# A transformer block on one core: the last shifted reading of a shared key tile, added in int32 pieces on GpSimd

## The chip, the core and the metric

The kernel runs on one core of a Trainium2 chip. The metric is the device time of one execution in microseconds. The engines are TensorE (PE in the profile; PEld is its weight load), VectorE (DVE), ScalarE (ACT), GpSimd (POOL) and SyncE (SP, which here only issues DMAs). "Lnnn" is a line of the kernel before.

## What is computed

The input is x, 2048 rows of 512 bfloat16 numbers, and a conditioning vector c. Two stages follow one another:

```python
mod = (_silu(c) @ w_mod)            # six vectors: sa, ca, ga, sb, cb, gb
h = _layernorm(x) * (1 + ca) + sa
x = x + ga * _A_ref(h, A_wqkv, A_wo)     # 32 heads of 16, softmax(q k^T / 4) v, then wo
h = _layernorm(x) * (1 + cb) + sb
x = x + gb * _B_ref(h, B_w1, B_b1, B_w2, B_b2)   # gelu(h w1 + b1) w2 + b2, F = 1376
```

Nearly all elementwise work is the softmax's exponential: 32 heads x 2048 queries x 2048 keys.

## The kernel before

**Units, tiles, runs.** Queries are cut into four blocks of 512, keys into 16 tiles of 128. A unit is one score product, 128 keys by 512 queries of one head (`qk`, L822). Four heads that lie in four row groups of TensorE go together: four units are a key tile of a run, and a run (32 of them) is four heads against all 16 key tiles of one query block. In the last query block a run takes eight heads and half of the queries, in pieces of 256 columns. The value products of a run (`pv_op`, L960) add into one PSUM bank `od`; when all are in, `normalise` copies it out (L985), sends the sums of the weights through DRAM to turn them round and invert them, and multiplies on GpSimd (L1012).

**Two ways to the exponential.** ScalarE takes units in turns of three and two (`qk_a`): the scores go to the PSUM tiles `st`, and one activation (L871) writes bfloat16 weights `pt`. Each tile then costs one value product. VectorE takes whole tiles, four of the 16 in each run (`DKS`; one in run 0), in another way (`qk_d`, `shifts`). Four passes (L912), one for each unit, read the scores from PSUM (`ax`), add a constant and write int16 numbers `ph`, whose bits read as bfloat16 are a rough exponential. Four shifts (L927) over all four units, 2048 columns, each add an integer step `PH_SH[j]` in SBUF and write `sh`: five readings in all, and a value product for each, with values scaled by `PH_W[j]` (`VX`), averages the error out. A tile that VectorE has not begun when ScalarE has done its own 12 goes to ScalarE (`next_tile`).

**The order.** Nothing runs in the order of the source. While the kernel is built, a planner (`Plan`, `Op`) keeps for each engine a list of operations with assumed times, latencies and priorities, and always emits the one that can start first; among those close together the lowest priority value goes (`dyn`), with a small scatter from `SEEDS`. That order is fixed in each engine's queue. `ahead` lets nothing on TensorE come in the way of the next scores for ScalarE. `heat` puts zero matmuls into gaps where less than `HEAT` us of products stand in the last 3.4 us. An operation marked `port` (shifts, some VectorE work in SBUF, GpSimd's work) is planned to start only when the other of VectorE and GpSimd is not in such an operation.

**GpSimd beside VectorE.** `beside` (L1043) makes the multiplications of L1012 and L1035 (weights scaled by a gate) run on GpSimd; it has them work in halves of 256 columns, which the planner admits only while VectorE is in an operation that is not marked `port`; `after_dve` makes it wait for the VectorE instruction before the latest one in the queue, so that it starts when the latest starts.

**Tail blocks.** After the last run of a query block `block_tail` does the output projection (L1117), the residual (L1166), the second layer norm, W1 (L1183) with its evictions on VectorE (L1193), one gelu over the block (L1202) and W2 (L1123). For the last block it takes only two row tiles of four, and the first 8 of 11 columns of W1 that way; the other three wait until all units are done and go through ScalarE's gelu out of PSUM (L1189). `last_half` does the other two row tiles when all runs are over: it loads x again (L491), transposes `od` on VectorE to find the divisors (L1249 to L1256), finishes the projection (L1263), and goes through the residual (L1267), statistics, W1 (L1295), gelu (L1298), W2 and the last addition (L1310), one row tile after the other.

Of the kernel before, what the change touches and what calls it, by code (L numbers as in the profile page):

```python
# [12 lines left out]
ALU = mybir.AluOpType  # L13
# [40 lines left out]
PEL = 0.24  # L54
OVER = 0.0
DVE_PE = 0.0
DL = 0.14
DPL = 0.08
AL = 0.17
FILL = 1.6  # L60
SPREAD = 0.15
SEEDS = (571, 338, 517, 702, 966, 607, 659, 937, 623, 185, 209, 513, 12, 512, 674, 785, 660, 579, 642, 245, 112, 195, 497, 319, 388, 80, 556, 716, 338, 990, 290, 195)
HEAT = 1.3
# [10 lines left out]
class Op:  # L74
    count = 0

    def __init__(self, eng, fn, us, deps=(), lat=0.14, prio=5.0, mode=None, kind="", acq=None,
                 rel=(), gate=None, port=False):
        self.port = port
        self.eng, self.fn, self.us, self.lat, self.prio = eng, fn, us, lat, prio  # L80
        self.mode, self.kind, self.acq, self.rel, self.gate = mode, kind, acq, rel, gate
        self.end = None
        self.ready = 0.0
        self.tile = None
        self.slot = None
        self.kb, self.due, self.extra = 0, 1e9, False
        self.uses = 0
        self.rows, self.cont, self.run = None, False, None
# [12 lines left out]
        for owner in rel:  # L101
            owner.uses += 1


class Plan:
# [56 lines left out]
    def ahead(self, can):  # L162
# [4 lines left out]
        limit = max(q[0][0], self.need() - q[0][1].us - PEL - 0.02) + OVER  # L167
# [90 lines left out]
def kernel(  # L258
# [34 lines left out]
    MM = 512 / 2400.0  # L293
# [55 lines left out]
    def dyn(plan, o):  # L349
        if o.eng == "DVE" and o.run is not None and (  # L350
                o.run < a_run[0] or o.run == a_run[0] and not own[o.run]):
            return 0.05
        if o.eng != "PE":
            return o.prio
# [14 lines left out]
        if o.kind == "last":  # L369
            return o.prio + 0.1 * same  # L370
        if o.due <= prog():
# [52 lines left out]
    warm = const.tile([P, P], BF16, name="warm")  # L424
    o_warm = op("POOL", lambda o: nc.gpsimd.memset(warm, 0.0), 0.2, prio=-1.0)
# [209 lines left out]
    def layer_norm(src, deps, mod, mod_dep, hold_z, alloc_h, engines, ps_res, kind, prio,  # L635
# [39 lines left out]
        else:  # L675
            for j in range(NC):
                def tr(o, j=j):
                    o.ps = o.tile.bitcast(BF16)[:, 0:nt * P]
                    for t in range(nt):
                        nc.tensor.transpose(out=o.ps[:, t * P:(t + 1) * P],  # L680
                                            in_=z.tile[:, t, j * P:(j + 1) * P], identity=ident)
                one = op("PE", tr, nt * 0.0705, za, lat=PEL, mode=("full", 0), kind=kind,
                         acq=r_ax, rel=(z,))
                trs.append(one)
                e = engines[j]
                done.append(op(e, lambda o, j=j, one=one, e=e: modulate(
                    e, h.tile[:, j, 0:nt * P], one.ps, mod, j), 0.13 + nt * 0.1, (one, mod_dep, h), prio=0.1,
                    rel=(one,)))
# [144 lines left out]
    def qk_a():  # L833
# [30 lines left out]
        o = op("PE", go, MM, deps, lat=PEL, mode=("qk",) + tuple(u[2] for u in got), kind="qkA", acq=r_st[n],  # L864
# [19 lines left out]
    def qk_d():  # L884
# [29 lines left out]
        d_e.append(op("DVE", ex, 0.61, (o,), lat=DL, prio=0.5, rel=(o,)))  # L914
# [7 lines left out]
    def shifts(r, kt, first, es):  # L922
# [3 lines left out]
        for j in range(1, NPH):  # L926
# [4 lines left out]
            pv_op(r, kt, j, (sh,), parts(sh), (sh,))  # L931

# [50 lines left out]
    def normalise(r):  # L983
# [20 lines left out]
        def d5(o):  # L1004
# [8 lines left out]
            out=OT.tile[:, c], in0=OD.tile[:, c], in1=o5.tile[:, c], op=ALU.mult), (OT,), (OD, o5))  # L1013
# [29 lines left out]
    def beside(fn, deps, rel=(), prio=0.5):  # L1043

        return [op("POOL", lambda o, c=c: after_dve(fn(slice(c * HB, (c + 1) * HB))), POOL_US, deps, lat=0.1,
# [107 lines left out]
    def block_tail(b, nt=TPB):  # L1153
# [19 lines left out]
        if part:  # L1173
            g.uses += 1
            o_late["part"] = g
            one = ones(g, (g,))
        ev = []
        over = op("NIL", None, 0.0, (), lat=0.0, prio=0.0, gate=finished) if part else None
        if part:
            open_banks()  # L1180
        for f in range(NF):
            direct = part and f >= PSUM_F
            mm = chain([(lambda ps, f=f, j=j: nc.tensor.matmul(  # L1183
                out=ps[:, 0:N], lhsT=W1[:, j, f * P:(f + 1) * P], rhs=h.tile[:, j, 0:N],
                start=(j == 0), stop=(j == NC - 1)), nt * MM / NC) for j in range(NC)],
                hd + [o_late["w1"], g, over if direct else None], kind,
                r_t if direct else r_ax, (h,))
            if direct:
                ev.append(op("ACT", lambda o, f=f, mm=mm: nc.scalar.activation(  # L1189
                    out=g.tile[0:rows(f), f, 0:N], in_=mm.tile[0:rows(f), 0:N], func=ACT.Gelu_apprx_tanh,  # L1190
                    bias=b1c[0:rows(f), f:f + 1], scale=1.0), 0.36, (mm,), lat=0.15, prio=0.4, rel=(mm,)))
                continue
            ev.append(op("DVE", lambda o, f=f, mm=mm: nc.vector.tensor_scalar(  # L1193
                out=g.tile[:, f, 0:N], in0=mm.tile[:, 0:N], scalar1=b1c[:, f:f + 1], scalar2=None,
                op0=ALU.add), 0.13 + nt * 0.134, (mm, o_late["b1"]), prio=0.3 if part else 0.1, rel=(mm,)))
# [13 lines left out]
        for t in range(nt):  # L1209
# [7 lines left out]
            dma(lambda o, t=t, a=a: nc.sync.dma_start(  # L1217
                out=out[0][b * QB + t * P:b * QB + (t + 1) * P, :], in_=a.tile), (a,), kb=128,
                rel=(a,))
        due(1e9)  # L1220


    def last_half():
        r, b = NR - 1, LAST
        full = ("full", 0)
        xr = load_x(b)
# [3 lines left out]
        x2 = xr  # L1230
        ln, z, h = take(r_ln, (x2,)), take(r_z, (x2,)), take(r_blk, (x2,))
        g = o_late["part"]
        od, OD, OT = o_od[r], take(r_OD), take(r_OT)
# [6 lines left out]
        s = None  # L1240
        for n, t in enumerate(tiles):
            den = work.tile([P, 8], FP32, name=f"den{t}")

# [3 lines left out]
            def turned(n):  # L1247
                return OD.tile[:, n * HB:(n + 1) * HB].rearrange("p (a q) -> p a q", a=2)
            sh = op("DVE", lambda o, t=t, half=half: nc.vector.transpose(out=turned(0), in_=half(od.tile)), 0.35,  # L1249
                    (o_last[r], OD, s), prio=0.06 + n)  # L1250
            rc = op("DVE", lambda o, den=den: nc.vector.reciprocal(
                out=den, in_=OD.tile[:, 16:HB:32]), 0.12, (sh,), prio=0.05 + n)
            bk = op("DVE", lambda o, den=den: nc.vector.transpose(
                out=turned(1).rearrange("p a q -> p (a q)"),
                in_=den.unsqueeze(2).to_broadcast([P, 8, 32])), 0.35, (rc,), prio=0.045 + n)
            ml = [op("DVE", lambda o, t=t, half=half: nc.vector.tensor_tensor(  # L1256
                out=half(OT.tile), in0=half(od.tile), in1=turned(1), op=ALU.mult),
                0.36, (bk, OT), prio=0.04 + n)]

            def wo2(o, t=t):  # L1260
                for p in range(2):
# [3 lines left out]
            w = op("PE", wo2, 2 * MM,  # L1265
                   ml + [early[t]], lat=PEL, mode=full, kind="last", prio=0.2)
            a = op("DVE", lambda o, t=t: nc.vector.tensor_tensor(  # L1267
                out=x2.tile[:, t, :], in0=acc[t].tile, in1=xr.tile[:, t, :], op=ALU.add), 0.62,
                (w, x2, xr), prio=0.024 + n / 50, rel=(acc[t],))
            s = op("DVE", lambda o, t=t: stats(ln, t, x2.tile[:, t, :]), 0.83, (a, ln), prio=0.022 + n / 50)  # L1270
            rs = op("POOL", lambda o, t=t: rstd(ln, t, t + 1), 0.9, (s,), prio=0.0)
            za = op("DVE", lambda o, t=t: apply(ln, z, t, x2.tile[:, t, :]), 0.33, (rs, z),
# [4 lines left out]
            for e in ("DVE", "ACT"):  # L1277
# [8 lines left out]
                for n, j in enumerate(js):  # L1286
                    hd.append(op(e, lambda o, n=n, j=j, e=e, at=at, tro=tro: modulate(
                        e, h.tile[:, j, at], tro.ps[:, n * P:(n + 1) * P], modB, j), 0.25, (tro, h),
                        prio=0.02, rel=(tro,)))
            gs = slice(HB + (t - 2) * P, HB + (t - 1) * P)  # L1290
            gd = []
            for f in range(NF):
                def w1(o, f=f, at=at):
# [3 lines left out]
                mm = op("PE", w1, 4 * 0.071, hd, lat=PEL, mode=full, kind="last", acq=r_t, prio=0.3)  # L1297
                gd.append(op("ACT", lambda o, f=f, mm=mm, gs=gs: nc.scalar.activation(  # L1298
                    out=g.tile[0:rows(f), f, gs], in_=mm.tile[0:rows(f), 0:P], func=ACT.Gelu_apprx_tanh,
                    bias=b1c[0:rows(f), f:f + 1], scale=1.0), 0.25, (mm,), prio=0.3, rel=(mm,)))  # L1300
            first = prev = None
            for f in range(NF):
                def w2(o, f=f, gs=gs):
                    w2_mm((first_of[id(o)] or o).tile, g.tile, gs.start, f, f + 1)
                o = op("PE", w2, MM, (gd[f], prev), lat=PEL if f == NF - 1 else 0.0, mode=full,
                       kind="last", acq=r_t if f == 0 else None, prio=0.4)
# [6 lines left out]
            dma(lambda o, t=t, a=a: nc.sync.dma_start(  # L1313
                out=out[0][b * QB + t * P:b * QB + (t + 1) * P, :], in_=a.tile), (a,), kb=128,
                rel=(a,))
# [137 lines left out]
```

## Time and profile before

| what | value |
|---|---|
| runs | 788.27 us median of 3 (787.38 to 789.58) |
| profiled execution, first to last instruction | 785.5 us |
| TensorE busy | 731.1 us (93%), 8209 matmuls |
| VectorE busy | 737.5 us (94%), 1285 instructions |
| ScalarE busy | 756.9 us (96%), 683 instructions |
| GpSimd busy | 125.0 us (16%), 279 instructions |
| share of the chain that ended last | ScalarE 42%, TensorE 29%, VectorE 14%, issue 12%, DMA 2% |
| end of the last exponential | 760.99 us |
| zero matmuls, L447, L431 | 11.2 us (116), 9.5 us (25) |

The profiled execution has no other time on record than its span; the median of the runs lies 2.8 us above it. In the page, a row such as `DVE 6779...` cuts the span into 40 slices of 19.6 us and gives the busy share of each in tenths. A group row has the line, the engine, what is written from what, the shapes, the count, the busy time and the mean length of one instruction, then the idle time in front of them and what ended it. A matmul's length includes its way through the array, and neighbours overlap; VectorE's and ScalarE's records overlap their neighbours too (a pass lasts 680 ns and the next one starts 600 ns after it).

### The profile page before, as it was taken

What the parts mean: (1) busy time and instruction counts of PE and PEld (TensorE: products, weight loads), DVE (VectorE), ACT (ScalarE), POOL (GpSimd) and SP (SyncE); (2) the same over time, 40 slices, a digit from 0 to 9 for tenths busy, and PEclk for the clock granted to TensorE, in tenths of its full rate; (3) what the DMA queues carried; (4) which work ended last, traced back from release to release, by engine and by line L of the source; (5) the groups of instructions that cost most, each with busy time, mean ns of one, the idle gap of its engine ahead of it and who ended that gap; (6) DMA issues with size and microseconds to landing.
All of it is one profiled execution on the core that took longest, in us unless ns stands there. A gap on an engine that the chain in (4) does not pass through costs nothing.

```text
span 785.5 us, 20448 instructions
## 1 busy us (share of the span) xinstructions
PE 731.1 (93%) x8209; PEld 272.8 (35%) x8286; DVE 737.5 (94%) x1285; ACT 756.9 (96%) x683; POOL 125.0 (16%) x279
## 2 busy tenths in 40 slices
PE   8899999999999898999998999999999999999897
PEld 3423333233333222223232233322234343344454
DVE  6779998999999999999999999999899999999974
ACT  4899999999999999999999999999999999999993
POOL 7420224121134300200002000001000100100100
PEclk9999999999999999999999999999999999999999
DMA  7042001001020010001000010001010000101010
GB/s 215 30 138 89 18 23 46 23 16 26 6 71 22 25 42 23 19 22 29 22 23 18 30 34 22 11 16 33 23 57 20 22 20 19 43 18 31 18 44 29
DMA packets 39073, 28.22 MB, mean 36 GB/s; under 512 B 17957, under 2 KB 34374, under 8 KB 38978
## 3 DMA queue, kind: packets, MB, share of 16 engines
q1 hardware_dynamic: 38970, 26.91, 12.0%
q8 instruction: 65, 1.06, 0.6%
q14 instruction: 30, 0.25, 0.1%
q10 hardware_dynamic: 8, 0.00, 0.0%
HBM read 21.30 MB, written 2.61 MB: 30 GB/s over the span
## 4 chain that ended last, share of the span: by engine, by line
ACT 42%; PE 29%; DVE 14%; issue 12%; DMA 2%; SPq 0%; POOL 0%; POOLq 0%; DVEq 0%; ACTq 0%
ACT pt L871 40%; PE od L960 9%; PE st L822 8%; DVE sh L927 6%; DVE ph L912 5%; PE ax L1123 2%; PE ax L822 2%; PE ax L1183 2%; ACT g L1202 1%; PE ax L701 1%; PE ax L431 1%; PE ax L740 1%; DVE ln_s L607 1%; DVE OD L985 1%; PE t L1123 1%
## 5 line engine op out<-in xcount | busy, mean ns | idle before, releaser
L871 ACT ACTIVATE pt<-st 128x1536 bf16<-128x1536 f32 x629 | 715.1, 1308 | 3.9 <-PE ax L822 1.7
L912 DVE TENSOR_SCALAR ph<-ax 128x512 int16<-128x512 f32 x476 | 311.1, 680 | 11.2 <-PE ax L822 9.7
L927 DVE TENSOR_SCALAR sh<-ph 128x2048 int16<-128x2048 int16 x476 | 310.8, 692 | 2.6 <-PE od L960 2.3
L822 PE MATMUL st<-qm,kT 32*128 32x512 bf16 x1572 | 246.8, 384 | 23.9 <-ACT pt L871 18.7
L822 PE MATMUL ax<-qm,kT 32*128 32x512 bf16 x476 | 167.0, 380 | 7.6 <-DVE ph L912 5.6
L960 PE MATMUL od<-sh,VX 128*32 128x512 bf16 (+1 forms) x2400 | 167.5, 340 | 5.4 <-DVE sh L927 4.6
L822 PEld LDWEIGHTS <-kT 32*128 32x128 bf16 x2048 | 81.1, 91 | 239.4 <-issue 230.6
L960 PE MATMUL od<-pt,VEB 128*32 128x512 bf16 (+1 forms) x1960 | 145.3, 342 | 0.3 <-ACT pt L871 0.3
L960 PEld LDWEIGHTS <-VX 128*32 128x32 bf16 x2400 | 60.5, 95 | 86.2 <-issue 75.3
L960 PEld LDWEIGHTS <-VEB 128*32 128x32 bf16 x2560 | 62.5, 96 | 75.6 <-issue 63.8
L1012 POOL TENSOR_TENSOR OT<-OD,RB 128x256 bf16<-128x256 f32 x38 | 27.2, 727 | 316.3 <-DVE sh L927 200.4
L960 PE MATMUL od<-ph,VEB 128*32 128x512 bf16 (+1 forms) x600 | 47.5, 340 | 1.7 <-DVE OD L985 1.4
L1012 POOL TENSOR_TENSOR OS<-OD,RB 128x256 bf16<-128x256 f32 x24 | 17.2, 727 | 156.7 <-DVE sh L927 111.0
L1183 PE MATMUL ax<-blk,W 128*128 128x512 bf16 (+1 forms) x145 | 39.8, 359 | 1.8 <-issue 0.6
L756 POOL TENSOR_SCALAR VX<-VEB 128x128 bf16<-128x128 bf16 x64 | 23.1, 360 | 80.7 <-DVE VEB L633 76.9
L701 PE MATMUL ax<-blk,w 128*128 128x512 bf16 x95 | 31.8, 382 | 3.7 <-DVE blk L626 0.9
L1123 PE MATMUL ax<-w,g 128*128 128x512 bf16 x100 | 29.2, 382 | 1.0 <-DVE ph L912 0.2
L1193 DVE TENSOR_SCALAR g<-ax,b1c 128x512 bf16<-128x512 f32 (+1 forms) x41 | 28.2, 692 | 1.1 <-PE ax L1183 0.7
L607 DVE BATCH_NORM_STATS2 ln_s<-xb 128x6 f32<-128x512 bf16 x32 | 21.6, 675 | 1.2 <-DMA xb<-in_A_x_dram 1.1
L1123 PEld LDWEIGHTS <-g 128*128 128x128 bf16 x176 | 14.0, 97 | 23.2 <-issue 12.7
L985 DVE COPY OD<-od 128x512 f32<-128x512 f32 x31 | 21.1, 681 | 0.7 <-issue 0.5
L1183 PEld LDWEIGHTS <-W 128*128 128x128 bf16 x176 | 14.0, 97 | 20.6 <-issue 14.9
(110 smaller groups left out, 367.5 us busy)
## 6 DMA issues: line engine op xcount, KB each, us to landing
RB<-rn SPq DMA_DIRECT2D x124, 64.0 KB
xb<-in_A_x_dram SPq DMA_DIRECT2D x8, 512.0 KB
out_dram<-o SPq DMA_DIRECT2D x16, 128.0 KB
qm<-qs SPq DMA_DIRECT2D x120, 16.0 KB
W<-in_B_w_dram SPq DMA_DIRECT2D x1, 1376.0 KB
w<-in_A_wqkv_dram SPq DMA_DIRECT2D x3, 384.0 KB
blk<-in_w_mod_dram SPq DMA_DIRECT2D x2, 512.0 KB
xb<-in_w_mod_dram SPq DMA_DIRECT2D x2, 512.0 KB
```

What stands on the lines that cost most here:

```text
L607: nc.vector.bn_stats(out=st6, in_=src)
L701: return chain([(lambda ps, j=j: nc.tensor.matmul(out=ps[:, 0:QB], lhsT=w.tile[:, j, cc * P:(cc + 1) * P], rhs=o_h[b].tile[:, j, :], start ...
L822: nc.tensor.matmul(out=o.tile[:, k * QB:(k + 1) * QB], lhsT=kT[cc][kb][rows, ko * P:(ko + 1) * P], rhs=qm.tile[rows, par, :] if hb is None ...
L871: nc.scalar.activation(out=e.tile[:, 0:len(got) * QB], in_=o.tile[:, 0:len(got) * QB], func=ACT.Exp, scale=ESC)
L912: nc.vector.tensor_scalar(out=ph.tile[:, o.row * QB:(o.row + 1) * QB], in0=o.tile, scalar1=PH_B, scalar2=0.0, op0=ALU.add, op1=ALU.max)
L927: sh = op("DVE", lambda o, j=j: nc.vector.tensor_scalar(out=o.tile, in0=first.tile, scalar1=PH_SH[j], scalar2=None, op0=ALU.add), 0.6, es, ...
L960: nc.tensor.matmul(out=o_od[r].tile[32 * i:32 * i + 32, n * HB:n * HB + w], lhsT=v_tile(kt, ph)[:, c0:c0 + 32], rhs=got[i][:, at:at + w], ...
L985: OD = op("DVE", lambda o: nc.vector.tensor_copy(out=o.tile, in_=od.tile), 0.6, (last,), prio=0.0, acq=r_OD, rel=(od,))
L1012: two = beside(lambda c: nc.gpsimd.tensor_tensor(out=OT.tile[:, c], in0=OD.tile[:, c], in1=o5.tile[:, c], op=ALU.mult), (OT,), (OD, o5))
L1123: nc.tensor.matmul(out=ps, lhsT=g[:, f, col:col + P], rhs=rhs, start=(f == 0), stop=(f == NF - 1))
L1183: mm = chain([(lambda ps, f=f, j=j: nc.tensor.matmul(out=ps[:, 0:N], lhsT=W1[:, j, f * P:(f + 1) * P], rhs=h.tile[:, j, 0:N], start=(j == ...
L1193: ev.append(op("DVE", lambda o, f=f, mm=mm: nc.vector.tensor_scalar(out=g.tile[:, f, 0:N], in0=mm.tile[:, 0:N], scalar1=b1c[:, f:f + 1], s ...
```

## The change

One of the four shifts of a VectorE tile, the last (`j = 4`), is no longer one VectorE instruction. `shared_reading` cuts it into four pieces of 512 int16 columns. GpSimd may add a piece as 256 int32 numbers, with the step in both halves of each (`PH_SH[-1] * 65537`); the planner admits a piece where `fits` finds a place beside VectorE's passes over PSUM. What GpSimd has not taken when VectorE comes to it, one VectorE instruction does (`rest`), late if a `ph` buffer is free and early if none is. TensorE's picks get a second filter, `fed`, which keeps other products from delaying VectorE's next scores.

Other parts go with it. The planner's assumed times of the exponentials now count to the end of the chain (`A_US`, `AL`, `PEA`), `HEAT` goes from 1.3 to 1.5, and the seeds are others. In tail blocks several transposes or W1 columns share a PSUM bank (only where fewer than 512 columns are used, for W1), and in the last block all 11 columns of W1 are done by VectorE's way before the runs end. `last_half` keeps the x tile that `block_tail` loaded, each of its two row tiles has an `OD` tile of its own, and the multiplication of the last run but one is not tied to a VectorE instruction.

```diff
+PEA = 0.38
 OVER = 0.0
+FEED = 0.2
...
-AL = 0.17
+AL = 0.055
...
-HEAT = 1.3
+HEAT = 1.5
...
-            can = self.ahead(can)
+            can = self.fed(self.ahead(can))
...
+    def fed(self, can):
+
+        q = [(s, o) for s, o in can if o.kind == "qkD"]
+        if not q:
+            return can
+        dry = self.free["DVE"] + sum(o.us for o in self.lists["DVE"])
+        limit = max(q[0][0], dry - q[0][1].us - PEL - DL) + FEED
+        return [(s, o) for s, o in can if o.kind in ("qkA", "qkD") or
+                s + o.us + (0.107 if o.mode[0] != "qk" else 0.0) <= limit]
...
+    def fits(self, us):
+
+        at, end, port = self.dve
+        t = max(at, self.now, self.free["POOL"])
+        if port and t < end:
+            return False
+        nxt = self.pick("DVE")
+        if nxt is None or nxt[0] - t >= us:
+            return True
+        if t >= end or nxt[0] > end + 0.15:
+            return not nxt[1].port and nxt[0] + nxt[1].us - t >= us
+        return end - t >= us or not nxt[1].port and nxt[0] + nxt[1].us - t >= us
...
-    A_US = {1: 0.49, 2: 0.92, 3: 1.345}
+    A_US = {1: 0.49, 2: 0.9165, 3: 1.3435}
+    PIECE = 0.74
+    REST = (4.0, 1.0)
+    PIECE_FIT = 0.6
...
-    PSUM_F = 8
+    PSUM_F = 11
...
+        if o.rest:
+            return REST[min(r_ph.free) > plan.now]
...
+    pair_sh = const.tile([P, 1], I32, name="pair_sh")
+    o_pair = op("POOL", lambda o: nc.gpsimd.memset(pair_sh, PH_SH[-1] * 65537), 0.1, prio=0.2)
...
-        for j in range(1, NPH):
+        shared_reading(r, kt, first, es)
+        for j in range(1, NPH - 1):
...
+    def shared_reading(r, kt, first, es):
+
+        sh = op("NIL", None, 0.0, es, lat=0.0, prio=0.0, acq=r_sh)
+        todo = [0, 1, 2, 3]
...
+        def add_pairs():
+            at = slice(todo[0] * QB, (todo[0] + 1) * QB)
+            del todo[:1]
+            return nc.gpsimd.tensor_tensor(out=sh.tile[:, at].bitcast(I32), in0=first.tile[:, at].bitcast(I32),
+                                           in1=pair_sh[:, 0:1].to_broadcast([P, HB]), op=ALU.add)
...
+        def part(o):
+            after_dve(add_pairs())
...
+        def rest(o):
+            o.us = (0.067, 0.2, 0.335, 0.47, 0.6)[len(todo)]
+            o.waiters.append(done)
+            add(len(todo))
+            drop()
...
+        mine = [op("POOL", part, PIECE, (sh, o_pair), lat=0.12, prio=0.8, kind="beside", port=True,
+               gate=lambda: plan.fits(PIECE_FIT)) for _ in range(4)]
+        q = op("DVE", rest, 0.6, (sh,), lat=DL, prio=2.0, port=True)
...
-            out=OT.tile[:, c], in0=OD.tile[:, c], in1=o5.tile[:, c], op=ALU.mult), (OT,), (OD, o5))
+            out=OT.tile[:, c], in0=OD.tile[:, c], in1=o5.tile[:, c], op=ALU.mult), (OT,), (OD, o5), free=r == NR - 2)
...
-        for f in range(NF):
-            direct = part and f >= PSUM_F
...
+        for f0 in range(0, NF, QB // N):
+            fs = range(f0, min(NF, f0 + QB // N))
...
-        xr = load_x(b)
+        x2 = held["x"]
...
-        s = None
         for n, t in enumerate(tiles):
             den = work.tile([P, 8], FP32, name=f"den{t}")
+            OD = take(r_OD)
```

More of the change, by code (lines that the diff above doesn't have):

```diff
@@ L87, in __init__ @@
         self.uses = 0
-        self.rows, self.cont, self.run = None, False, None
+        self.rows, self.cont, self.run, self.rest = None, False, None, False
         self.waiters = []
@@ L370, in dyn @@
             return o.prio + 0.1 * same
+        if o.cont:
+            return 0.9 + same
         if o.due <= prog():
@@ L1041, in w2_scaled, with beside @@
                       gb_bc, (W2[0], W2[1], o_late["small"], o_late["gb"]))
-    def beside(fn, deps, rel=(), prio=0.5):
+    def beside(fn, deps, rel=(), prio=0.5, free=False):
+        if free:
+            return [op("POOL", lambda o, c=c: fn(slice(c * HB, (c + 1) * HB)), POOL_US, deps, lat=0.1, prio=0.1,
+                       rel=rel, port=True) for c in range(2)]
         return [op("POOL", lambda o, c=c: after_dve(fn(slice(c * HB, (c + 1) * HB))), POOL_US, deps, lat=0.1,
@@ L1312, in last_half @@
                 acq=r_o, rel=(first,))
-            dma(lambda o, t=t, a=a: nc.sync.dma_start(
-                out=out[0][b * QB + t * P:b * QB + (t + 1) * P, :], in_=a.tile), (a,), kb=128,
-                rel=(a,))
+            store(b, t, a)
     first_of = {}
```

134 lines of the change are left out of this document (77 added, 57 removed).

## Prediction

> **What bounds the kernel now.** I read the page first: busy shares, the row of slices, the costliest groups.
>
> ```profile
> PE   8899999999999898999998999999999999999897
> DVE  6779998999999999999999999999899999999974
> ACT  4899999999999999999999999999999999999993
> L871 ACT ACTIVATE pt<-st 128x1536 bf16<-128x1536 f32 x629 | 715.1, 1308 | 3.9 <-PE ax L822 1.7
> L912 DVE TENSOR_SCALAR ph<-ax 128x512 int16<-128x512 f32 x476 | 311.1, 680 | 11.2 <-PE ax L822 9.7
> L927 DVE TENSOR_SCALAR sh<-ph 128x2048 int16<-128x2048 int16 x476 | 310.8, 692 | 2.6 <-PE od L960 2.3
> L822 PE MATMUL st<-qm,kT 32*128 32x512 bf16 x1572 | 246.8, 384 | 23.9 <-ACT pt L871 18.7
> ```
>
> ScalarE (ACT) is full from the second slice to the last but one, and its exponentials wait 3.9 us in all: **the exponentials on ScalarE set the end**, behind a head and a tail. VectorE (DVE) is just as full, and the two share one stock of work: 2048 units of 512 columns, four to a key tile. ScalarE does 1572 (715.1 us, 0.455 us each, 1.82 us a tile), VectorE 476, that is 119 tiles, each with four passes over PSUM (L912) and four shifts (L927): 621.9 / 119 = 5.23 us. Only 4 tiles of a run (one in the first run) may go to VectorE, 31 x 4 + 1 = 125. Six went back to ScalarE because VectorE was late; counting the loads of the scaled values between the ends of runs, they lie scattered, one run at a time. So a faster VectorE is worth **at most 6 x 1.82 = 10.9 us**, however much it is relieved.
>
> Then the timeline, where GpSimd (POOL) already multiplies 256 columns beside a pass:
>
> ```profile
> 155.07 0.68 DVE L912 TENSOR_SCALAR ph<-ax 128x512 int16<-128x512 f32 x1
> 155.24 0.73 POOL L1012 TENSOR_TENSOR OT<-OD,RB 128x256 bf16<-128x256 f32 x1 [16.53 <-DVE sh L927]
> 155.68 0.84 DVE L927 TENSOR_SCALAR sh<-ph 128x2048 int16<-128x2048 int16 x1
> 156.44 0.68 DVE L912 TENSOR_SCALAR ph<-ax 128x512 int16<-128x512 f32 x1
> ```
>
> The pass is untouched (0.68 us beside POOL as elsewhere); the shift behind it takes 0.84 us instead of 0.68, because POOL's 0.73 us reach over the pass's end. That is the price to watch.
>
> Last, the chain of waits behind the last exponential (it ends at 760.99 us):
>
> ```profile
> 758.76 1.43 POOL OT L1012 x2
> ...
> 762.67 3.80 DMA xb<-in_A_x_dram
> ...
> 766.59 0.70 DVE xb L1267
> ...
> 771.72 0.70 DVE xb L1267
> ...
> 776.09 2.63 PE t L1295 x44
> 778.73 0.05 issue
> 778.78 3.20 PE t L1123 x14
> ```
>
> Here 24.5 us lie outside ScalarE's bound: the multiply comes late, the x load is queued behind its DMAs on SP's queue, and the first addition (766.59) waits for the load.
>
> **The change, part by part.** Everything is set against the span of 785.5 us; the median of the runs, 788.27, lies 2.8 above it, and I add 2.8 at the end.
>
> *The fifth reading.* Per tile it removes one shift, 0.60 us of VectorE by the starts of neighbouring instructions, and puts up to four pieces of 256 int32 columns on POOL and one instruction for what is left on VectorE. No row shows an int32 add. The nearest are L1012 (727 ns, two float32 inputs) and L1035 (671 to 736 ns, bf16), both 256 columns with two inputs; I take 727, with bounds of 671 and, for the doubled output bytes, 1454. POOL is busy 125 us of 785.5, and 476 pieces would add 346: there is room. What costs is VectorE's wait. Of the 476 passes, 181 are followed at once by a shift and 198 by another pass; a piece in front of a second pass is free, one in front of a shift costs 0.16 to 0.21 us (837 and 893 ns against 680). Over what POOL does beside passes today (62 + 34 instructions at L1012 and L1035), 55 shifts average 112 ns longer: 6.2 us, 64 ns a piece. No row shows a quarter shift either: between 0.15 us (a quarter of 0.60) and 0.32 (the pitch of L618, 512 columns in SBUF); I take 0.20. If three pieces of four find a place, a tile saves 600 - 200 - 3 x 64 = 208 ns; bounds: 600 (all four, free) and 600 - 320 - 3 x 155 = -185. Over 119 tiles: **24.8 us of VectorE, from 71 down to -22**. I choose the middle because pieces want four passes a tile and find about five, 96 of all passes being taken by the older multiplies.
>
> *What that buys.* Below, three more evictions cost VectorE 1.4 us. (24.8 - 1.4) / 5.2 = 4.5 of the six tiles come back: **4.5 x 1.82 = 8.2 us** off ScalarE; bounds 10.9 gained and 22 / 5.2 x 1.82 = 7.7 lost. TensorE (PE) pays four more value products per tile, 4 x 0.39 us: 7 us inside its 54 us of idle time.
>
> *The wait that is added.* TensorE's value product of the fifth reading now waits for POOL or for the rest. Behind it on TensorE stand the next score products, and ScalarE waits for those. Today such waits on shifts come to 4.6 us in 17 cases (0.27 each) and ScalarE's exponentials lose 3.2 us to TensorE. 119 times 0.27 would be 32 us of TensorE; ScalarE has two score tiles in hand (0.92 and 1.34 us of work), which cover 0.27. I take nothing, with a bound of another 3.2 us. The pending reading also holds one of four buffers for shifts; VectorE waits 2.3 us for those today, and passes stand in.
>
> *More zero matmuls, new latencies.* The granted clock is 1.00 in every window from 60 us on, so nothing is to be won there; between 40 and 60 us it is 0.91, but ScalarE is busy 19.75 of the 20. Zero products at L447 and L431 take 20.7 us; half as many again stays inside TensorE's idle time. Nothing, with a bound of 1 us either way for a score product that stands behind one. The constant's memset on POOL costs 0.25 us by L553's rows, in the head; I take nothing. The latencies and seeds only reorder, and ScalarE's 3.9 us of waiting bound a gain.
>
> *The tail.* Three of eleven W1 products (12 matmuls, 1.48 us at 761.38) move ahead of the last exponential: TensorE has cover there, VectorE pays 3 x 0.478 = 1.4 us. The second x load goes, and the multiply of the last run but one no longer waits for a place. The first addition can then stand behind its product (OT's multiply, L1256, ends at 763.16, two products take 0.6), about 764.0 instead of 766.59; the second half's transposes no longer wait for the first's statistics, so its addition can come 3 us earlier too. What is late next is TensorE: from 761.38 to 781.98 it is idle only some 1.8 us. Without the 1.48 us it can end at most 1.48 + 1.8 = 3.3 us earlier. I take **2.0 us**, between nothing and 3.3, since the first W2 products still wait for the gelu.
>
> Sum: 785.5 - 8.2 - 2.0 = 775.3 us; with 2.8, **778.1**.
>
> **Rivals.**
> - *VectorE ceases to matter.* If pieces sit mostly in rows of passes, all six tiles return: 785.5 - 10.9 - 2.5 + 2.8 = 774.9. For it: 198 passes followed by a pass already, more of them with a quarter fewer shifts. Against: evictions of the tail blocks fall into bursts in which six late tiles arose.
> - *The relief doesn't arrive.* Pieces end late, the rest runs on VectorE, and only the tail is left: 785.5 - 2.0 + 2.8 = 786.3. For it: VectorE has hardly any idle time in which to be early, and a run's tiles can't be begun much ahead. Against: a saved 0.6 us needs no gap.
> - *Slower: the port.* If pieces fall in front of shifts, each holds VectorE 155 ns or more, as at 155.68. With three pieces and a rest of 0.20, the break-even is 400 / 3 = 133 ns a piece: above it VectorE loses tiles. At the bound, 4.2 tiles go to ScalarE: 785.5 + 7.7 - 2.0 + 2.8 = 794.0. A longer int32 add leads there too: 130 ns over 727 on each isolated piece passes break-even. For it: 181 passes stand before a shift, and 155 is over 133. Against: 64 ns on average today. [...]
>
> **How the numbers follow.** Forecast 0.47, all six tiles 0.25, tail alone 0.11, port 0.17. A measurement here tells some 0.3% (2.4 us) from no change. Faster: 0.47 + 0.25 + 0.03 of the tail's case (786.3 lies within 2.0 of 788.3) = 0.75; same 0.08; slower 0.17. The range leaves out the port case but for its edge, and little below 774.9: 773 to 789. The forecast's own range is 775.5 to 784.
>
> **What would show it.** Exponentials: ACT units down from 1572 towards 1554 (1548 at the cap), passes up from 476 towards 494 (500), busy time of L871 near 707. Shifts (L927's like) near three a tile, with a new POOL group of some 300 to 400 pieces near 730 ns. Shifts beside POOL no longer than 64 ns a piece on average. ScalarE's idle time unchanged between 60 us and the last exponential. In the tail no x load, first addition within 3 us of the last value product, and the end about 22 us after the last exponential. The prediction is wrong if passes do not rise above 480, if the mean shift rises above 0.80 us, if the int32 add takes over 0.9 us, or if ScalarE's waits for TensorE grow past 6 us.

## The result, and the profile after

The changed kernel takes 784.29 us (median of 4 runs, 781.98 to 784.9) against 788.48 us of the kernel before on the same chip (787.38 to 789.58): a ratio of 0.9947, 95% interval 0.993 to 0.9964. It is faster by 4.2 us; 10.2 were forecast. A repetition of the same program on another chip, told below, gave 781.86 us and a ratio of 0.9913 (0.989 to 0.9937), 7.1 us. In the profiled executions the span went from 785.5 to 782.9 us.

The page of the changed kernel, the rows that answer to those of before (line numbers have moved: L871 is L905, L912 is L946, L927 is L962; L978 is the rest on VectorE, L984 the piece on GpSimd):

```profile
PE 730.8 (93%) x8315; PEld 271.3 (35%) x8395; DVE 722.6 (92%) x1269; ACT 752.0 (96%) x677; POOL 256.6 (33%) x492
PE   8889999999999999999999999999999999999997
DVE  6789989999999999999999999999987999998984
ACT  4999999999999999999999999999999999999994
L905 ACT ACTIVATE pt<-st 128x1536 bf16<-128x1536 f32 x626 | 710.7, 1325 | 7.6 <-PE st L856 3.8
L946 DVE TENSOR_SCALAR ph<-ax 128x512 int16<-128x512 f32 x484 | 315.8, 681 | 25.3 <-PE ax L856 23.1
L962 DVE TENSOR_SCALAR sh<-ph 128x2048 int16<-128x2048 int16 x363 | 242.4, 700 | 2.0 <-PE od L1044 1.2
L984 POOL TENSOR_TENSOR sh<-ph,pair_sh 128x256 int32<-128x256 int32 x212 | 128.8, 616 | 280.6 <-DVE sh L962 190.4
L978 DVE TENSOR_SCALAR sh<-ph 128x2048 int16<-128x2048 int16 (+3 forms) x86 | 50.7, 594 | 0.4 <-PE od L1044 0.3
```

Passes went from 476 to 484: **two tiles came back, not four and a half**. GpSimd took 212 pieces. VectorE's busy time fell from 737.5 to 722.6 us although it does two tiles more, and its row has lost nines: its idle time rose from 48.0 to 60.3 us of the span, so a good half of what it was relieved of was not used. The waits say what it waited for; first the kernel before, then the changed one (waited for: us in total, times, longest):

```profile
DVE ph L912 <- PE ax L822: 9.7, 21, 1.3
```

```profile
DVE ph L946 <- PE ax L856: 23.1, 36, 4.5
```

VectorE now waits 13 us more for scores that TensorE has not yet made for it.

How pieces look beside passes, in the timeline of the changed kernel (start, length, engine, line):

```profile
139.33 0.79 DVE L962 TENSOR_SCALAR sh<-ph 128x2048 int16<-128x2048 int16 x1
140.04 2.54 DVE L946 TENSOR_SCALAR ph<-ax 128x512 int16<-128x512 f32 x4
140.29 3.05 POOL L984 TENSOR_TENSOR sh<-ph,pair_sh 128x256 int32<-128x256 int32 x5 [0.72 <-DVE sh L962]
142.50 0.68 DVE L1069 COPY OD<-od 128x512 f32<-128x512 f32 x1
```

Five pieces lie beside four passes and a copy out of PSUM, which start 0.60 to 0.66 us apart (two passes in a row: 0.60 in the median of the trace). (The shift in front, 0.79 us, overlaps an older multiply of GpSimd, from 138.90 to 139.57 us; shifts beside none last 0.68.)

The tail, in the chain that ended last:

```profile
764.00 2.12 PE ax L1210 x9
766.11 0.43 PE t L1350 x2
...
769.14 1.79 PE t L1381 x32
...
775.89 3.42 PE ax L1210 x15
779.31 0.02 issue
779.33 0.69 DVE o L1396
```

No load stands in it any more. From the end of the last exponential (760.0 us) to the end it is 22.9 us instead of 24.5.

The accounts of the two profiled executions, from the rows and from the first and the last exponential: exponentials -4.4 us, ScalarE's idle time between its first and last exponential +2.5 (5.6 to 8.1), a later first exponential +0.6, other work of ScalarE +0.3, tail -1.6: together -2.6, as the spans say.

### The profile page after: what moved, and what is told of

The parts are those of the page before. It is cut to its first block, busy times and chain, and to the rows that moved or that the text cites. A ratio compares the mean times of both kernels' runs of the same rounds, so it can differ in the third digit from the quotient of the medians.

```text
span 782.9 us, 20900 instructions
## 1 busy us (share of the span) xinstructions
PE 730.8 (93%) x8315; PEld 271.3 (35%) x8395; DVE 722.6 (92%) x1269; ACT 752.0 (96%) x677; POOL 256.6 (33%) x492
## 4 chain that ended last, share of the span: by engine, by line
ACT 37%; PE 34%; DVE 16%; issue 10%; DMA 2%; POOL 1%; SPq 0%; DVEq 0%; POOLq 0%; ACTq 0%
ACT pt L905 35%; PE od L1044 12%; PE st L856 10%; DVE ph L946 7%; DVE sh L962 4%; PE ax L1210 4%; PE ax L1271 3%; PE ax L856 2%; PE ax L735 1%; DMA blk<-in_w_mod_dram 1%; ACT g L1286 1%; PE t L1381 1%; DVE sh L978 1%; PE od L481 1%; DVE g L1276 1%
## 5 line engine op out<-in xcount | busy, mean ns | idle before, releaser
L905 ACT ACTIVATE pt<-st 128x1536 bf16<-128x1536 f32 x626 | 710.7, 1325 | 7.6 <-PE st L856 3.8
L946 DVE TENSOR_SCALAR ph<-ax 128x512 int16<-128x512 f32 x484 | 315.8, 681 | 25.3 <-PE ax L856 23.1
L962 DVE TENSOR_SCALAR sh<-ph 128x2048 int16<-128x2048 int16 x363 | 242.4, 700 | 2.0 <-PE od L1044 1.2
L984 POOL TENSOR_TENSOR sh<-ph,pair_sh 128x256 int32<-128x256 int32 x212 | 128.8, 616 | 280.6 <-DVE sh L962 190.4
L1044 PE MATMUL od<-sh,VX 128*32 128x512 bf16 (+1 forms) x2432 | 172.5, 342 | 1.7 <-DVE sh L962 0.7
L856 PE MATMUL ax<-qm,kT 32*128 32x512 bf16 x484 | 165.2, 380 | 7.3 <-DVE ph L946 4.3
L1044 PE MATMUL od<-pt,VEB 128*32 128x512 bf16 (+1 forms) x1952 | 142.7, 342 | 0.7 <-DVE OD L1069 0.5
L1096 POOL TENSOR_TENSOR OT<-OD,RB 128x256 bf16<-128x256 f32 x38 | 29.0, 774 | 72.7 <-DVE sh L962 60.1
L978 DVE TENSOR_SCALAR sh<-ph 128x2048 int16<-128x2048 int16 (+3 forms) x86 | 50.7, 594 | 0.4 <-PE od L1044 0.3
L1271 PE MATMUL ax<-blk,W 128*128 128x512 bf16 (+1 forms) x155 | 41.5, 352 | 1.7 <-issue 0.5
L1210 PE MATMUL ax<-w,g 128*128 128x512 bf16 x115 | 32.4, 381 | 2.2 <-ACT g L1281 1.1
L1210 PEld LDWEIGHTS <-g 128*128 128x128 bf16 x176 | 14.1, 97 | 24.5 <-issue 11.9
```

The source lines that it names most:

```text
L856: nc.tensor.matmul(out=o.tile[:, k * QB:(k + 1) * QB], lhsT=kT[cc][kb][rows, ko * P:(ko + 1) * P], rhs=qm.tile[rows, par, :] if hb is None ...
L905: nc.scalar.activation(out=e.tile[:, 0:len(got) * QB], in_=o.tile[:, 0:len(got) * QB], func=ACT.Exp, scale=ESC)
L946: nc.vector.tensor_scalar(out=ph.tile[:, o.row * QB:(o.row + 1) * QB], in0=o.tile, scalar1=PH_B, scalar2=0.0, op0=ALU.add, op1=ALU.max)
L962: sh = op("DVE", lambda o, j=j: nc.vector.tensor_scalar(out=o.tile, in0=first.tile, scalar1=PH_SH[j], scalar2=None, op0=ALU.add), 0.6, es, ...
L978: return nc.vector.tensor_scalar(out=sh.tile[:, at], in0=first.tile[:, at], scalar1=PH_SH[-1], scalar2=None, op0=ALU.add)
L984: return nc.gpsimd.tensor_tensor(out=sh.tile[:, at].bitcast(I32), in0=first.tile[:, at].bitcast(I32), in1=pair_sh[:, 0:1].to_broadcast([P, ...
```

## The experiments

Three theories stood at the start. *Relief* is the prediction's: tiles follow from VectorE's time, and the relief is too small. *Order*: the order that the planner builds, which the scatter from the seeds and the rules of the early runs shape, decides where a tile is lost. *Wait*: readings that come late hold up TensorE, and ScalarE with it. Seeds matter because they scatter the planner's priorities; the scatter also takes the line number of an operation, so edits were made without moving lines. The kernel before ran beside each group on the same chip; the medians of it were 789.01 (first group), 790.56 (second), 788.11 (third) and 788.97 us (fourth).

**Equal seeds, with and without pieces.** Each list of seeds is drawn at random and given to the kernel before, the changed kernel, and (two lists) the changed kernel without pieces:

```diff
-SEEDS = (327, 149, 358, ...
+SEEDS = (788, 861, 82, ...
```

and for the last kind also

```diff
-               gate=lambda: plan.fits(PIECE_FIT)) for _ in range(4)]
+               gate=lambda: False) for _ in range(4)]
-    REST = (4.0, 1.0)
+    REST = (2.0, 2.0)
```

> The kernel before with another list of 32 seeds, drawn at random; nothing else. Order theory: how many tiles VectorE gets depends on the order that the scatter happens to give, and the seeds of the kernel before gave it an order better than most; with others VectorE gets 117 to 118 tiles (468 to 472 passes) and the time is 4 to 8 us longer, 792 to 796 us. Relief theory (tiles follow from VectorE's time alone): 476 passes as before within 4, and the time within 2 us of the kernel before.

> The changed kernel with the same random seeds as the run before it. Order theory: 119 to 120 tiles, 4 to 6 us slower than the changed kernel (788 to 790 us), and 5 to 8 us faster than the kernel before with these seeds. Relief theory: 484 passes and 784 us as the changed kernel, 4 us faster than the kernel before with these seeds. Wait theory (fifth readings that come late from GpSimd hold up TensorE, and ScalarE with it): ScalarE idles 2 us or more beyond the kernel before with these seeds.

> The changed kernel with the same random seeds, in which GpSimd takes no piece: VectorE adds the whole fifth reading in one instruction with the priority of the other shifts; all else of the change stays. Order theory: 117 tiles (468 passes), 4 to 7 us slower than with pieces and the same seeds, and 0 to 3 us faster than the kernel before with these seeds (tail and latencies). Relief theory: the same direction, 208 ns a tile or 25 us of VectorE, 4.5 tiles, 8 us slower than with pieces. Wait theory: less idle time of ScalarE than with pieces.

> The kernel before with a second list of random seeds. Order theory: 116 to 118 tiles (464 to 472 passes) and 793 to 798 us, as with the first random list. Chance alternative (the first random list was an unlucky one): 119 tiles and 788 to 790 us.

> The changed kernel with the second list of random seeds. Order theory: 119 to 120 tiles, 788 to 792 us, and 4 to 8 us faster than the kernel before with the same list. Relief theory as on record, with the seeds without effect: 784 us.

> The changed kernel with the second random list, and GpSimd takes no piece (VectorE adds the whole fifth reading in one instruction). Order theory: 116 to 117 tiles, within 3 us of the kernel before with the same list, and 4 to 8 us slower than with pieces. Rival (the rest of the change does it, not the pieces): within 2 us of the run with pieces.

> The kernel before with a third list of random seeds. Order theory: 117 tiles (468 passes), 793 to 798 us.

> The changed kernel with the third list of random seeds. Order theory: 119 to 120 tiles, 787 to 790 us, 4 to 8 us faster than the kernel before with this list; so the mean gain at equal seeds over three lists is 5 to 8 us, more than the 4.2 us between the two kernels with their own seeds.

| seeds | before | changed, no pieces | changed |
|---|---|---|---|
| own | 788.48 us, 119 tiles | not tried | 784.29 us, 121 tiles |
| first list | 797.35, 118 | 796.78, 117 | 789.63, 120 |
| second list | 794.28, 117 | 804.85, 116 | 789.80, 119 |
| third list | 802.32, 117 | not tried | 785.59, 120 |

Against the kernel before with its own seeds the three lower rows read, from left to right, 1.011 (1.0065 to 1.0155), 1.0094 (1.0079 to 1.0109), 1.0014 (0.9988 to 1.004); 1.006 (1.0032 to 1.0087), 1.0171 (1.0138 to 1.0205), 1.0006 (0.9988 to 1.0024); and 1.0173 (1.0117 to 1.0228) and 0.9961 (0.9938 to 0.9983). The kernel before came out slower than expected with the first and the third list (1 and 4 us above the ranges), the changed kernel faster with the third (1 us below). The passes and pieces of the first list, changed kernel:

```profile
L946 DVE TENSOR_SCALAR ph<-ax 128x512 int16<-128x512 f32 x480 | 313.0, 681 | 31.3 <-PE ax L856 29.7
L984 POOL TENSOR_TENSOR sh<-ph,pair_sh 128x256 int32<-128x256 int32 x207 | 125.0, 612 | 255.3 <-DVE sh L962 172.1
```

Three things follow. Random seeds make the kernel before 6 to 14 us slower than its own and the changed kernel 1 to 6 us: relief theory's "no effect" falls. Pieces are worth three tiles in both lists that tell (117 to 120, 116 to 119) and 7.2 and 15.1 us; without them the change is no gain (-0.6 and +10.6 us; the second had been expected within 3 us of the kernel before). And at equal seeds the changed kernel gets two, two and three tiles more than the kernel before and is 7.7, 4.5 and 16.7 us faster. So lucky seeds of the kernel before had not hidden tiles: two to three is what the change brings with all four lists. They had hidden time: the mean gain over the three random lists is 9.6 us, above the 5 to 8 expected and the 4.2 with own seeds.

These gains are not tiles alone. With the third list the profiled span is 14.1 us shorter: 7.3 us of exponentials, 5.0 of tail and 4.1 of ScalarE's idle time, while the first exponential came 2.7 us later. With the second list the pieces take 14.0 us off the span, and half of that is idle time of ScalarE (14.6 us without pieces, 7.3 with); the execution without pieces also had the lower clock (0.989 against 0.998). The wait theory is not needed: with the first list ScalarE's idle time was 6.5 us with pieces and 9.1 without.

**The fifth reading for nothing.** The addition is left out on both engines, and the value product takes the first reading again:

```diff
-            add(len(todo))
+            del todo[:]
...
-               gate=lambda: plan.fits(PIECE_FIT)) for _ in range(4)]
+               gate=lambda: False) for _ in range(4)]
-        q = op("DVE", rest, 0.6, (sh,), lat=DL, prio=2.0, port=True)
+        q = op("NIL", rest, 0.0, (sh,), lat=0.0, prio=0.0)
...
-        src = lambda: [sh.tile[:, h * QB:(h + 1) * QB].bitcast(BF16) for h in range(4)]
+        src = lambda: [first.tile[:, h * QB:(h + 1) * QB].bitcast(BF16) for h in range(4)]
```

> The changed kernel, in which the fifth reading's addition is left out altogether: its value product takes the first reading again, so that neither GpSimd nor VectorE spends time on it. Relief theory: VectorE is relieved of 0.6 us in each tile, 70 us in all, so all six tiles come back: 500 passes, and 774 us or less. Order theory: three tiles at most, 488 to 492 passes, because single tiles of the early runs are lost to rules of the order while VectorE waits; VectorE's busy time falls below 690 us without ScalarE's units going along; 780 to 783 us.

Measured 783.97 us, 0.9919 (0.9895 to 0.9943), 122 tiles: the tiles that order theory expected, 1 us above its time. The page, with the engines' busy times:

```profile
PE 738.9 (94%) x8456; PEld 271.5 (35%) x8456; DVE 684.6 (87%) x1190; ACT 750.8 (96%) x675; POOL 128.1 (16%) x280
...
L905 ACT ACTIVATE pt<-st 128x1536 bf16<-128x1536 f32 x624 | 709.4, 1322 | 8.6 <-PE st L856 4.9
L946 DVE TENSOR_SCALAR ph<-ax 128x512 int16<-128x512 f32 x488 | 319.4, 681 | 43.4 <-PE ax L856 41.5
```

This decides against the prediction's step. VectorE is idle 98 us (782.9 - 684.6) and waits 41.5 us for scores, and still only three of six tiles are back. Which ones can be counted in the traces, by the value products between the copies of `od` that end the runs. The kernel before has one tile of four less in each of the runs 3, 4, 7, 15, 20 and 27, the changed kernel in 3, 4, 15 and 28, this one in 2, 3 and 4. From run 5 on nothing is lost any more; what is left lies in the early runs, although VectorE is idle 18.7 us in runs 1 to 4.

**The rule of the early runs.** In `before` and after, VectorE may begin a run ahead of ScalarE only once ScalarE is past run 3. First changed on top of the missing addition, then with the whole work in place (and one seed of 32 another):

```diff
-                                             and d_run() <= a_run[0] + (a_run[0] > 3))):
+                                             and d_run() <= a_run[0] + (a_run[0] > -1))):
```

> The changed kernel without the fifth reading's addition (its value product takes the first reading again), and with one rule of the order changed: VectorE may begin a run before ScalarE from the first run on, not from the fifth on. Order theory: the tiles that were still missing without the addition (runs 2 to 4) belong to this rule and not to VectorE's time; now 123 to 124 tiles (492 to 496 passes), ScalarE's exponentials 3 to 4 us less than without the addition alone, and 779 to 782 us. Rival (something else in the early runs, such as scores that TensorE delivers late): 122 tiles as before the rule was changed.

> The changed kernel with the whole addition of the fifth reading, with the early rule changed (VectorE may begin a run before ScalarE from the first run on) and one seed of the 32 another. Order theory: the order built so has 121 tiles (484 passes) too, so within 2 us of the changed kernel, 782 to 786 us, and the lost tiles lie in other runs. Rival (the rule was what cost the tiles, and with it gone 123 return): 492 passes and 780 us.

Without the addition: 783.28 us, 0.9927 (0.9898 to 0.9955), and 124 tiles.

```profile
L905 ACT ACTIVATE pt<-st 128x1536 bf16<-128x1536 f32 (+1 forms) x621 | 706.5, 1309 | 8.8 <-PE ax L856 3.6
L946 DVE TENSOR_SCALAR ph<-ax 128x512 int16<-128x512 f32 x496 | 323.6, 684 | 31.2 <-PE ax L856 28.7
```

Two more tiles (run 8 alone now lacks one), 2.9 us fewer of exponentials. The time expected, 779 to 782 us, was missed: the median is only 0.7 us below the last one, on another chip, and against the kernel before beside it there is no gain (0.9927, 0.9919 without the rule's change). With the work in place: 783.68 us, 0.993 (0.9906 to 0.9954), 484 passes, as the changed kernel, with a tile less in runs 3, 5, 8 and 27. So the rule holds tiles back when VectorE has time, but its change does not by itself bring any.

**Pieces anywhere.** GpSimd may take a piece whenever it is planned free and VectorE is in no operation marked `port`:

```diff
-               gate=lambda: plan.fits(PIECE_FIT)) for _ in range(4)]
+               gate=lambda: True) for _ in range(4)]
```

> The changed kernel, in which GpSimd takes a piece at any time that its queue and the shared port are planned to be free, not only where it fits beside passes over PSUM. Port theory (a piece in front of a shift holds VectorE up for what it reaches beyond the pass, 0.16 us and more, against the 0.13 us of VectorE that it saves): 318 pieces instead of 212, shifts beside GpSimd much longer than 0.68 us on average, fewer tiles than 121, and 789 us or more. Rival (the port costs little; more pieces are more relief): 484 passes or more and 784 us or less.

Measured 795.9 us, 1.0081 (1.0053 to 1.0108), 119 tiles.

```profile
L946 DVE TENSOR_SCALAR ph<-ax 128x512 int16<-128x512 f32 x476 | 310.7, 683 | 35.4 <-PE ax L856 31.9
L984 POOL TENSOR_TENSOR sh<-ph,pair_sh 128x256 int32<-128x256 int32 x318 | 193.8, 621 | 273.1 <-DVE sh L962 116.1
L962 DVE TENSOR_SCALAR sh<-ph 128x2048 int16<-128x2048 int16 x357 | 242.8, 719 | 3.1 <-PE od L1044 2.4
```

Half as many pieces again, two tiles fewer, 11 to 12 us slower: more pieces are not more relief. But whole shifts that overlap an instruction of GpSimd are long only by 12.4 us in all (114 of them, 793 ns on average) against 7.5 us in the changed kernel (78, 778 ns). So the longer shifts cost VectorE 5 us more, and it waits 8.8 us more for scores (31.9 against 23.1) in an order built around the pieces. Of the 9.1 us by which the span is longer, 3.8 are exponentials, 4.6 idle time of ScalarE and 0.9 tail. The expectation had the direction and the time, not the means; and with one list of seeds it is not shown how much of the loss comes from the longer shifts and how much from the other order.

**The clock.** In the profiled execution of the changed kernel, TensorE's clock was at half for 3.4 us from 307.6 and from 317.8 us. Two experiments: zero matmuls added that the planner does not count, in an otherwise equal order, and the same program again.

```diff
-            if o.extra:
+            if o.extra or left[r] > 0 and sum(u for t, u in plan.done if t > plan.now - 3.4) < 2.0:
                 zeros(r)
```

> The changed kernel with its own seeds and its own planned order, instruction for instruction, to which zero matmuls are added that the planner does not count: after a value product, wherever the products of the last 3.4 us planned come to less than 2.0 us (132 groups of four). Clock theory: two of the four microseconds that the changed kernel has not gained by its two tiles are ScalarE's idle time behind half-clock windows at 308 and 318 us; with more zeros these windows go, ScalarE's idle time between the first and the last exponential falls from 8.1 to below 6.5 us, and the time to 782 us or less. Rival: each group takes 0.2 us of TensorE in front of score products, ScalarE waits more for TensorE, and the time rises by 1 us or more.

> The changed kernel unchanged, to see whether the half-clock windows at 308 and 318 us and ScalarE's 2.2 us of idle time beside them come again. Clock theory (the windows cost those 2.2 us): where the windows are missing, ScalarE's idle time between the first and the last exponential is near 6 us instead of 8.1; where they are there, near 8. Rival (the idle time there belongs to the order of the instructions and would be there at full clock): near 8 us with and without the windows.

With more zeros: 795.54 us, 1.0063 (1.0039 to 1.0087), and a half-clock stretch at 322 us all the same. ScalarE's waits there:

```profile
ACT pt L905 <- PE ax L856: 7.3, 14, 1.7
ACT pt L905 <- PE st L856: 4.8, 12, 0.7
```

The rival is right: 132 groups of zeros are added, ScalarE waits more for scores, and its idle time went from 8.1 to 14.5 us. This kernel can't tell what the half-clock stretches cost. The repetition can: 781.86 us, 0.9913 (0.989 to 0.9937). The stretches of 5 us (PE, PEld, VectorE, ScalarE and GpSimd busy, granted clock), first in the first profile, then in the repetition:

```profile
305.00:310.00 5.00, 4.09 (x40) 1.16 (x39) 4.46 (x9) 4.67 (x5) 0.00 (x0) 0.76 0.14 32
310.00:315.00 5.00, 4.81 (x54) 1.19 (x51) 4.71 (x9) 4.36 (x4) 1.41 (x2) 0.90 0.07 25
315.00:320.00 5.00, 4.09 (x41) 1.16 (x37) 4.79 (x8) 4.89 (x5) 3.07 (x5) 0.78 0.05 13
320.00:325.00 5.00, 5.00 (x65) 1.41 (x58) 3.61 (x6) 3.87 (x4) 0.00 (x0) 0.88 0.02 3
```

```profile
305.00:310.00 5.00, 3.98 (x51) 1.34 (x50) 5.00 (x10) 5.00 (x6) 0.30 (x1) 1.00 0.09 28
310.00:315.00 5.00, 4.28 (x45) 1.23 (x43) 5.00 (x9) 5.00 (x6) 1.44 (x3) 1.00 0.10 29
315.00:320.00 5.00, 4.39 (x59) 1.63 (x62) 4.81 (x9) 5.00 (x6) 2.69 (x5) 1.00 0.05 15
320.00:325.00 5.00, 4.95 (x54) 1.41 (x44) 5.00 (x10) 5.00 (x5) 0.00 (x0) 1.00 0.02 2
```

ScalarE loses 0.33 + 0.64 + 0.11 + 1.13 = 2.2 us in the first and nothing in the second; its idle time between the exponentials is 8.1 us in one and 5.4 in the other, the span 782.9 and 780.0. The order of the instructions is the same and the clock is not, and the waits lie in the two stretches. All ten runs of the changed kernel say the same: the five with a mean clock of 0.997 or 0.998 and the one with 0.999 took 781.39 to 782.73 us, the four with 0.993 or 0.995 took 783.84 to 784.9. So the clock cost those 2.2 us. Each of the two stretches lasted 3.41 us. In the 3.4 us before them the array had products for some 0.42 and 0.49 of the time (estimates from the products' columns and starts; a product of 512 columns is counted as 0.21 us; groups of them that follow one another at full clock start 0.216 us apart in the median of the trace). In the repetition the same places have some 0.44 and 0.52 (estimated in the same way), and no half clock follows; no run here shows what halves the clock, or at which share.

## Why the prediction was wrong, point by point

**The direction and the range held; the size was two and a half times too large.** The step that failed is *what that buys*, "(24.8 - 1.4) / 5.2 = 4.5 of the six tiles come back": two came back, and the exponentials fell by 4.4 us instead of 8.2. In the first profile the span fell by 2.6 us instead of 10.2; of the 7.6 that are missing, 3.8 are this term, 2.5 are ScalarE's idle time, for which nothing was forecast, 0.9 the later first exponential and other work of ScalarE, and 0.4 the tail.

- *The relief itself* was met: VectorE's passes, shifts and rests take 608.9 / 121 = 5.03 us a tile instead of 5.23; 194 ns were saved, 208 forecast. That is luck, for two errors cancel in it. Pieces were 1.75 a tile (212 / 121), not three; 35 tiles were done wholly by GpSimd, 39 of 86 rests were whole shifts. But they cost less: 612 ns in the median, not 727, and of 212 only 23 had a shift or a rest as VectorE's next instruction, so that shifts beside GpSimd grew by 7.5 us in all, against 6.1 before. The quarter shift, guessed at 0.20 us, is 283 ns long as recorded, 0.20 without the 80 ns that neighbours overlap.
- *From relief to tiles* it went wrong. I divided VectorE's freed time by a tile's cost, as if time freed anywhere could be used anywhere. Of the 23 us that the change freed (119 x 0.194), 10 went into two tiles, and VectorE's idle time grew by 12. A tile goes back to ScalarE because VectorE is late in that run, and time freed in others turns into waiting for scores.
- *Six tiles to bring back*: I had read the six losses as one kind, and they are of two. Two of them lay in runs 3 and 4. The fifth reading for nothing took 71 us of shifts away (119 x 0.60) and left three losses, in runs 2 to 4 (in run 2 anew); these went when the rule of the early runs was changed too. The page of before held the warning: VectorE already waited 9.7 us for scores, and it was idle 2.3 and 2.0 us in runs 3 and 4. The other four losses, from run 5 on, do go with VectorE's time: four before, two in the changed kernel, none with the fifth reading for nothing. But there too the division is too generous. The 104 tiles from run 5 on were relieved of 20 us, which would be 3.9 tiles, and two came; VectorE's idle time between the ends of runs 4 and 30 rose from 12.1 to 25.3 us (23.2 in the repetition). These counts are of one order each; with the first list of seeds the pieces brought back tiles of runs 2 and 4 as well.
- *Seeds and latencies*: "only reorder", with a gain bounded by ScalarE's 3.9 us of waiting. That bound counts waiting alone, and seeds move tiles too: random ones took one to two tiles from the kernel before and made it 6 to 14 us slower. That the mean gain at equal seeds, 9.6 us, lies near the 10.2 forecast does not bear out the sum: its exponentials fell by 4.6, 4.2 and 7.3 us, with two, two and three tiles.
- *Nothing for the zero matmuls, within 1 us*: the bound was too narrow, because it took the clock for fixed. TensorE was granted 1.00 from 60 us on in the one profile I had, and I took that for settled. Half-clock stretches cost the profiled run 2.2 us, and the repetition, with fewer, is 7.1 us below the kernel before. The same holds for the kernel before: in the last group its runs go from 785.92 us at a mean clock of 1.0 to 792.0 at 0.987. Runs of that group with a clock of 0.997 or more average 787.3 us before and 781.9 after, so at like clocks the change is worth 5.4 us; part of the difference between 4.2 and 7.1 is chance.
- *The tail*: 2.0 forecast, 1.6 measured (1.7 in the repetition). The first addition stands 3.1 us behind the last exponential (763.13), 3.0 forecast; the second at 767.42 instead of 771.72. TensorE's idle time from 761.38 to 781.98 us is 1.5 us in the trace of before, not 1.8, so the bound of 3.3 should have been 3.0; and the first rival takes 2.5 us off the tail where the sum takes 2.0.
- *The wait for the fifth reading*: nothing forecast, and TensorE's waits on VectorE's shifts fell (value products of 512 columns: 4.4 to 0.7 us, of 5.1 and 1.5 us of idle time before them). One of the signs of being wrong did appear: ScalarE's exponentials waited 7.0 us for TensorE (3.8 + 3.2), past the 6 named. In the repetition it was 4.2 (2.4 + 1.8), so the excess went with the clock, not with the reading.
- *The rival "the port"* did not come, because the planner keeps pieces away from shifts (the 23 of 212 above). Where pieces may go anywhere, the kernel is slower than before (795.9 us), as the rival says; that the longer shifts alone do it is not shown (they cost VectorE 5 us more, and the kernel is 11 to 12 us slower).

By the repetition's profile, the change is worth -4.54 us of exponentials, -1.67 of tail and +0.75 of the rest: 5.5 us of span. What decides each tile lost from run 5 on is left open: the one rule tried brought no tiles back with the work in place. No version tried that does the whole work is shown to beat the changed kernel.

## What to carry to other kernels

When two engines share a stock of work by an order fixed in advance, freed time on one of them is worth only what it does in the runs in which that engine was late: look at each run that lost work, and at the engine's idle time in it, before dividing totals. Compare such kernels over several seeds of the order; here one seed list against another can be worth more than the change, and several experiments above have only one. A kernel whose clock differs from one execution to the next (0.993 to 0.999 on average in the ten runs of the changed kernel) needs several profiles before a 2 us difference is explained.

## What the hardware showed that was not expected

An int32 add of 256 columns on GpSimd, one input a constant column, took 612 ns in the median; float32 inputs and a bfloat16 output took 730 for the same columns, bfloat16 ones 675. It is thus cheaper than the nearest row, although it writes twice the bytes. The five pieces at 140.29 us start 0.61 us apart on average, about the pitch of the passes (0.60), beside four passes and a copy out of PSUM. A pass that overlaps an instruction of GpSimd lasts 680 ns on average (326 of 484), the others 684.

TensorE's clock was halved for 3.41 us at two places in one execution of a program and not in the next, after stretches in which its array had products for some 0.42 and 0.49 of the time (estimates, see above); this kernel, whose end ScalarE sets, lost 2.2 us to them. The zero matmuls added against them cost more than that: with 132 groups the span was 11 us longer (793.9 against 782.9), and one half-clock stretch was there all the same.
